# The last two chunks of the last expert's weight go into the first token tiles by a path of their own; filler matmuls, one program body per engine, fifteen small extra loads

## The chip, the core and the metric

The kernel runs on one core of one Trainium2 chip. Its engines are TensorE (PE in the profile; PEld is its weight loads), VectorE (DVE), ScalarE (ACT), GpSimd (POOL) and SyncE (SP), each with a program of its own. Data move between HBM and the on-chip memory SBUF by sixteen DMA engines. Loads are issued by POOL (queue q0 in the profile), the stores of the result by SP (queue q1), and programs are fetched over queue q8. The metric is the device time in microseconds of one execution; lower is better.

## The reference, cut to what matters

Attention comes first, then a mixture of experts in which 32 slots (8 experts of 4) each take a softmax-weighted mean of all 4608 tokens, and each token takes a softmax-weighted mean of the 32 slots' outputs.

```python
x = attention(q, k, v)                  # [4608, 512]: sliding window in heads 0-3, dilated in 4-7
logits = x @ phi                        # [4608, 32]
d = softmax(logits, over tokens)
slot_input = (d.T @ x).reshape(8, 4, 512)
for e in range(8):
    h = relu(slot_input[e] @ w1[e])     # [4, 1024]
    slot_out[e] = h @ w2[e]             # [4, 512]
c = softmax(logits, over the 32 slots)
out = c @ slot_out                      # [4608, 512]
```

## The kernel before

The kernel is written as a list of operations, each with its engine, what it reads and writes, a guessed cost and a key. `Prog.schedule` orders them on a model of the engines: at each step it takes the engine that can start first and, of that engine's operations that could start within 0.12 us of the earliest, the one with the lowest key. POOL and SP keep the order in which the operations were written. `Prog.emit` then walks that order and writes each engine's program, with semaphore waits where an operand comes from elsewhere; before the change, each operation is a body of its own, opened by a decorator call.

Attention runs over 8 units `u` (two batches by one kind of head each). POOL loads q, k, v of a unit with a cast to bf16 (line 396), PE transposes them (lines 520, 525), ACT copies them to `TT` (L544), and scores, exponentials, masks and products follow (L562 to L657). After each second unit come the logits (L671), their exponentials `expT` (slots on 128 partitions, tokens along them; L676) and the slots' sums in the PSUM bank `psA`, bank 7 of eight (L715). The pool `psum` hands out the other seven banks, singly or in three pairs.

The sixteen weights `w10`..`w17`, `w20`..`w27` (each 2 MB in float32, 1 MB as stored in bf16) are loaded by POOL too (`wload`, L425), into buffers `WD`, then into `stg` and `TT` once those are free. The last, `w27`, is loaded in two parts, row chunks 0 to 5 and 6 and 7 of its eight chunks: a chunk has 128 of the 1024 rows, one on each partition, and all 512 columns.

The last stage is a chain. `psA` is copied and folded (L757, L762, L767), the first expert layer is 64 matmuls of 512 columns (L782), ReLU gives `h_sb` (L789, L792), eight transposes and four copies give `hT` (L800, L809). Row sums for the second softmax come from L819 and `rtok` (L824). The second layer, L840, accumulates each expert's four slots in a PSUM pair `sp_`, 32 output partitions for a pair of experts, in two halves of 256 columns. `so_sb` is its scaled copy (L854 on DVE, L858 on ACT). Then 18 tiles of 256 tokens each: two matmuls of 512 columns (L879), one scaled copy each on ACT (L882) and DVE (L885) to a float32 buffer laid over old weight buffers, and one store of 512 KB by SP (L890).

`filler(n)` makes an operation of `n` matmuls of 512 columns whose result nobody reads. `schedule` may place one where PE's model is idle for over 0.4 us within the stretch `FILL`, in model time. `FILL = (125.0, 0)` is an empty stretch.

Of the kernel before, what the change touches and what calls it, by code (L numbers as in the profile page):

```python
# [22 lines left out]
HALO = 32  # L23
FILL = (125.0, 0)

# [84 lines left out]
class Prog:  # L110
# [6 lines left out]
    def op(self, e, fn, r=(), w=(), a=(), alloc=(), cost=0.5, key=0.0, mode="f",  # L117
           sem=None, nbytes=0, after=()):
        o = Op(e, fn, cost, key, mode)
        deps = list(after)  # L120
        for b in r:
            deps += b.ready
        for b in w:
            b.fresh()
            deps += b.prev
        for b in a:
            deps += b.prev
        seen = set()
        for d in deps:
            if d.id not in seen:  # L130
                seen.add(d.id)
                o.deps.append(d)
        for b in r:
            b.reads.append(o)
        for b in list(w) + list(a):
            b.ready.append(o)
        o.wr = [b for b in list(w) + list(a) if b.pool is not None]
        for b in list(r) + list(w) + list(a):
            if b.pool is not None and b not in o.touch:
                b.left += 1  # L140
                o.touch.append(b)
        o.alloc = list(alloc)
        o.sems = sem
        o.bytes = nbytes
        self.ops.append(o)
        return o
# [102 lines left out]
    def emit(self, nc, eng_of):  # L249
        ctr = {e: [nc.alloc_semaphore("c_" + e), 0] for e in ("pe", "act", "dve", "pool", "sp")}  # L250
        known = {e: {} for e in ctr}
        for o in self.order:

            @eng_of[o.e]
            def _(eng, o=o):
                e = o.e
                evs = {}
                hist = [h for t in o.wr for h in t.hist]
                for d in o.deps + hist:
                    if d.e == e == "pe":  # L260
                        continue
                    sem, val = d.ev
                    if val > evs.get(sem.num, (None, 0, None))[1]:
                        evs[sem.num] = (sem, val, d)
                if e == "pool" and o.sems is None and ctr[e][1]:
                    evs[ctr[e][0].num] = (ctr[e][0], ctr[e][1], None)
                kn = known[e]
                todo = sorted(evs.values(), key=lambda x: -(x[2].end if x[2] is not None else 0))
                for sem, val, d in todo:
                    if kn.get(sem.num, 0) >= val:  # L270
                        continue
                    eng.wait_ge(sem, val)
                    kn[sem.num] = max(kn.get(sem.num, 0), val)
                    if d is not None:
                        for k_, v_ in d.snap.items():
                            if kn.get(k_, 0) < v_:
                                kn[k_] = v_
                inst = o.fn(eng)
                if o.sems is not None:
                    for i_ in inst:  # L280
                        i_.then_inc(o.sems.sem, 16)
                        o.sems.val += 16
                    o.ev = (o.sems.sem, o.sems.val)
                else:
                    inst.then_inc(ctr[e][0], 1)
                    ctr[e][1] += 1
                    o.ev = (ctr[e][0], ctr[e][1])
                o.snap = dict(kn)
                o.snap[o.ev[0].num] = o.ev[1]


def bass_dilated_sliding_attn__then__soft_moe_slots_kernel(
# [14 lines left out]
    def sb(name, shape, dt=BF16):  # L307
        return A(nc.sbuf_tensor(name, shape, dt))

    NPT, NVN, NXB, NXT, NET = 6, 5, 5, 4, 2  # L310
    WD = sb("WD", [128, 7, 4096])
    stg = sb("stg", [128, 3, 9216])
# [23 lines left out]
    hT = sb("hT", [128, 2, 8, 4, 32])  # L336
    so_sb = sb("so_sb", [128, DM])

    ps = A(nc.psum_tensor("ps", [128, 8, 512], F32))
# [3 lines left out]
    one = [[i] for i in range(7)]  # L343
    psum = Pool(7, {1: [[6]] + one[:6], 2: [[0, 1], [2, 3], [4, 5]]})

# [7 lines left out]
    def tile(pool, size=1):  # L353
        t = Buf(pool)
        t.size = size
        return t

    def sbt(t):
# [20 lines left out]
    b_expT, b_expX = [Buf() for _ in range(B)], Buf()  # L379
    b_siT, b_h, b_hT, b_so = Buf(), [Buf(), Buf()], [Buf(), Buf()], [Buf(), Buf()]  # L380

    PACE = 13.1
# [4 lines left out]
    def load_unit(u):  # L387
        bp, ty, s = u // 2, u % 2, u % 3

        def f(g):  # L390
# [8 lines left out]
            return res  # L399
        op("pool", f, w=[b_stg[s]], cost=3.5, sem=s_u[s], nbytes=96 * 2 * 4608 * 4)  # L400

# [259 lines left out]
    def st_L(b, u):  # L661
# [49 lines left out]
        def pe3(t):  # L711
# [7 lines left out]
            return i_  # L719
        op("pe", pe3, r=[et, xb0, xb1], a=[b_acc], cost=0.35, mode="c", key=k0 + 4.0)  # L720

# [28 lines left out]
    wload("w26")  # L750
    wload("w27", ((0, 6), (6, 8)))

# [3 lines left out]
    op("dve", lambda vv: vv.reciprocal(rcs[:], rcs[:]), w=[b_rcs], cost=0.1, key=K1)  # L756
    op("dve", lambda vv: vv.tensor_copy(psA_sb[:], psA), r=[b_acc], w=[b_psA], cost=0.65, key=K1)  # L757
    fo = tile(psum, 1)
# [57 lines left out]
    def rsum(t):  # L816
# [8 lines left out]
       cost=0.2, key=K1 + 1)  # L825

    sp_ = tile(psum, 2)
    b_sp = [Buf(), Buf()]
    first = True
    for es_ in ((0, 1, 2, 3), (4, 5, 6), (7,)):  # L830
        for lo, hi_ in ((0, 6), (6, 8)):
            for h_ in range(2):
                pbs = [pb for e in es_ for l2, h2, pb in HOME[f"w2{e}"][1].parts
                       if l2 < hi_ and h2 > lo]

                def pe(t, es_=es_, lo=lo, hi_=hi_, h_=h_):
                    for cc in range(lo, hi_):
                        for e in es_:
                            j, hi = e % 4, e // 4
                            i_ = t.matmul(pair(sp_)[32 * j:32 * j + 32, h_, 0:256],  # L840
                                          hT[:, hi, cc, j, :],
                                          w2v[e][:, cc, 256 * h_:256 * h_ + 256],
                                          start=(hi == 0 and cc == 0), stop=(hi == 1 and cc == 7))
                    return i_
                last_ = op("pe", pe, r=[b_hT[0], b_hT[1]] + pbs, alloc=[sp_] if first else [],
                           a=[sp_, b_sp[h_]], cost=0.12 * (hi_ - lo), mode="c",
                           key=K1 + 2 + es_[0] + (0.5 * h_ + 0.2 * (lo > 0)))
                for e in es_:
                    HOME[f"w2{e}"][1].reads.append(last_)
                first = False  # L850
    for h_ in range(2):
        sl = slice(256 * h_, 256 * h_ + 256)
        if h_ == 0:
            op("dve", lambda vv, sl=sl: vv.tensor_scalar(so_sb[:, sl], pair(sp_)[:, 0, 0:256],  # L854
                                                         rcs[:, 0:1], None, op0=AluOp.mult),
               r=[b_sp[0], b_rcs], w=[b_so[0]], cost=0.35, key=K1 + 20)
        else:
            op("act", lambda ac, sl=sl: ac.activation(so_sb[:, sl], pair(sp_)[:, 1, 0:256],  # L858
                                                      ACTF.Copy, scale=rcs[:, 0:1]),
               r=[b_sp[1], b_rcs], w=[b_so[1]], cost=0.4, key=K1 + 20)  # L860

    for o_ in P.ops[-2:]:
        o_.touch.append(sp_)
        sp_.left += 1

    osts = []
    for ap, b in b_home[:9]:
        t32 = ap.bitcast(F32).rearrange("p (n j f) -> p n j f", n=2, j=2)
        for n_ in range(2):
            osts.append((t32[:, n_], b))  # L870
    for o in range(NOG):
        po = tile(psum, 2)
        ost, hb = osts[o]
        ob = Buf()
        ob.prev = list(hb.ready + hb.reads)

        def pe(t, o=o, po=po):
            for j in range(2):
                i_ = t.matmul(pair(po)[:, j, :], tok[o][:, j], so_sb[:], start=True, stop=True)  # L879
            return i_  # L880
        op("pe", pe, r=b_so + b_expT, w=[po], alloc=[po], cost=0.45, key=K1 + 30 + o)
        op("act", lambda ac, o=o, po=po, ost=ost: ac.activation(  # L882
            ost[:, 0, :], pair(po)[:, 0, :], ACTF.Copy, scale=rtok[:, 2 * o:2 * o + 1]),
            r=[po, b_rtok], a=[ob], after=ob.prev, cost=0.6, key=K1 + 30 + o)
        op("dve", lambda vv, o=o, po=po, ost=ost: vv.tensor_scalar(  # L885
            ost[:, 1, :], pair(po)[:, 1, :], rtok[:, 2 * o + 1:2 * o + 2], None,
            op0=AluOp.mult), r=[po, b_rtok], a=[ob], after=ob.prev, cost=0.6, key=K1 + 30 + o)
        so = DmaSem(nc, f"s_out{o}")
        s_out.append(so)
        op("sp", lambda e, o=o, ost=ost: [e.dma_start(  # L890
            out[256 * o:256 * o + 256, :].rearrange("(p j) f -> p j f", j=2), ost)],
            r=[ob], cost=0.1, sem=so, nbytes=524288, key=K1 + 30 + o)

# [58 lines left out]
```

## Time and profile before

| | |
|---|---|
| Device time, median of 3 runs | 183.03 us (182.87 to 183.22) |
| Profiled execution, its own span, first to last instruction | 181.2 us |
| Around the span, by the median | 1.8 us |
| Mean granted clock of TensorE | 0.922 |
| Busy: PE, PEld, DVE, ACT, POOL | 128.8, 96.6, 112.9, 93.1, 35.8 us |
| Read from HBM, written to it | 61.93 MB, 9.44 MB |

Times in the profile are microseconds from the start of the span. A profile page shows busy shares in forty equal slices, the DMA queues, the chain of work that ended last (each step followed back to what released it), and groups of instructions by source line. No time of the profiled execution beyond its span is recorded, so the median stands for it. Bytes in the DMA rows are counted as stored: a load that casts float32 to bf16 reads twice what they show.

### The profile page before, as it was taken

Reading aid. Unit: us, or ns where it says so; the run is one execution under the profiler, and the core shown is the slowest. Engines: PE = TensorE matmul, PEld = TensorE weight load, DVE = VectorE, ACT = ScalarE, POOL = GpSimd, SP = SyncE. Lnnn points to the kernel's source line nnn. Section 1 sums busy time; section 2 is a strip of 40 time slices with the busy share of each in tenths; the row PEclk is TensorE's granted clock in tenths of the full one; section 3 lists DMA queues with packets and bytes.
Section 4 is the critical chain, followed back from the end, with each engine's and each line's share of the span. In section 5 each row is a group of like instructions: output and inputs, shape, how many; then the busy total and the mean of one; then the engine's idle time right before and its main releaser. Section 6 shows DMA issues by size and latency. Waiting matters only on the chain.

```text
span 181.2 us, 5690 instructions
## 1 busy us (share of the span) xinstructions
PE 128.8 (71%) x2551; PEld 96.6 (53%) x2552; DVE 112.9 (62%) x257; ACT 93.1 (51%) x135; POOL 35.8 (20%) x72
## 2 busy tenths in 40 slices
PE   0018868877988988988887998876958984993000
PEld 0018658665778777778766767755544573210000
DVE  6830794893687799687599579699430201996000
ACT  2006867953775975775785765682400101995000
POOL 7990704303400700800200200204000000000000
PEclk9999999998899999999999999998795799998555
DMA  5999999999999999999999999999999981699995
GB/s 80 210 208 220 207 219 212 216 215 216 221 203 218 208 222 208 219 211 218 212 212 220 208 221 212 217 217 215 219 212 219 211 171 23 242 400 404 408 403 230
DMA packets 7896, 40.80 MB, mean 225 GB/s; under 512 B 1856, under 2 KB 1856, under 8 KB 4416
## 3 DMA queue, kind: packets, MB, share of 16 engines
q0 software_dynamic: 4752, 30.94, 82.6%
q1 hardware_dynamic: 3120, 9.50, 13.4%
q8 instruction: 20, 0.33, 0.7%
q14 instruction: 4, 0.03, 0.0%
HBM read 61.93 MB, written 9.44 MB: 394 GB/s over the span
## 4 chain that ended last, share of the span: by engine, by line
DVE 26%; DMA 25%; PE 23%; ACT 8%; POOL 6%; issue 3%; DVEq 0%; POOLq 0%
DMA TT<-in_moe_w_dram 15%; DMA stg<-in_v_dram 10%; DVE XB L627 8%; DVE PT L577 6%; DVE WD L885 5%; ACT PT L569 5%; POOL stg L396 4%; PE ps L671 4%; PE ps L520 3%; DVE VN L592 3%; PE ps L587 3%; PE ps L525 3%; PE ps L562 2%; PE ps L644 2%; ACT TT L544 2%
## 5 line engine op out<-in xcount | busy, mean ns | idle before, releaser
L544 ACT ACTIVATE TT<-ps 128x864 f32<-128x864 f32 x32 | 28.5, 894 | 31.4 <-PE ps L525 22.5
L569 ACT ACTIVATE PT<-ps 128x768 bf16<-128x768 f32 x48 | 36.6, 815 | 5.7 <-PE ps L562 5.4
L627 DVE TENSOR_TENSOR XB<-ps,RV 96x768 bf16<-96x768 f32 x32 | 30.3, 947 | 0.7
L525 PE MATMUL ps<-ident,stg 96*64 96x96 bf16 x576 | 17.0, 219 | 17.5 <-DMA stg<-in_v_dram 13.2
L525 PEld LDWEIGHTS ps<-ident,stg 96*64 96x64 bf16 x576 | 14.9, 119 | 19.1 <-DMA stg<-in_v_dram 13.4
L592 DVE COPY VN<-ps 128x768 bf16<-128x768 bf16 x32 | 17.6, 548 | 9.6 <-PE ps L587 9.5
L616 PE MATMUL ps<-VN,PT 128*128 128x65 bf16 x384 | 17.6, 194 | 2.9 <-DVE PT L577 1.4
L656 DVE COPY XT<-ps 128x576 bf16<-128x576 bf16 x17 | 10.1, 596 | 12.2 <-PE ps L644 12.1
L396 POOL DMA_DIRECT2D stg<-in_q_dram x16 | 8.4, 528 | 45.3 <-PE ps L525 23.3
L616 PEld LDWEIGHTS ps<-VN,PT 128*128 128x128 bf16 x384 | 14.3, 98 | 5.5 <-DVE PT L577 2.0
L587 PE MATMUL ps<-ident,TT 128*128 128x128 bf16 x192 | 16.5, 224 | 0.7 <-DVE VN L592 0.5
L562 PE MATMUL ps<-TT 64*128 64x96 bf16 x384 | 15.4, 205 | 2.1 <-ACT TT L544 1.0
L644 PE MATMUL ps<-ident,XB 96*128 96x96 bf16 x192 | 13.6, 215 | 3.6 <-DVE XB L627 3.6
L520 PE MATMUL ps<-ident,stg 96*128 96x96 bf16 x288 | 14.9, 206 | 0.1
L577 DVE TENSOR_TENSOR PT<-PT,mask_d 128x768 bf16<-128x768 bf16 x24 | 13.0, 545 | 1.1 <-ACT PT L569 0.6
L644 PEld LDWEIGHTS ps<-ident,XB 96*128 96x128 bf16 x192 | 10.5, 103 | 5.9 <-DVE XB L627 4.9
L587 PEld LDWEIGHTS ps<-ident,TT 128*128 128x128 bf16 x192 | 11.1, 99 | 4.5 <-DVE VN L592 1.4
L520 PEld LDWEIGHTS ps<-ident,stg 96*128 96x128 bf16 x288 | 13.0, 98 | 0.3 <-ACT PT L569 0.3
L562 PEld LDWEIGHTS ps<-TT 64*128 64x128 bf16 x384 | 9.7, 95 | 5.9 <-ACT PT L569 1.4
L577 DVE TENSOR_TENSOR PT<-PT,mask_p 128x768 bf16<-128x768 bf16 x24 | 12.6, 539 | 0.0
L657 ACT ACTIVATE XT<-ps 128x576 bf16<-128x576 bf16 x15 | 9.8, 650 | 3.6 <-PE ps L644 3.3
L879 PE MATMUL ps<-so_sb,expT 128*128 128x512 bf16 x35 | 10.3, 384 | 1.5 <-ACT so_sb L858 0.8
(75 smaller groups left out, 165.2 us busy)
## 6 DMA issues: line engine op xcount, KB each, us to landing
WD<-in_moe_w_dram POOLq DMA_DIRECT2D x7, 1024.0 KB, 27.6
out_dram<-WD SPq DMA_DIRECT2D x14, 512.0 KB, 6.4
stg<-in_moe_w_dram POOLq DMA_DIRECT2D x6, 1024.0 KB, 22.7
stg<-in_q_dram POOLq DMA_DIRECT2D x16, 288.0 KB, 17.1
stg<-in_k_dram POOLq DMA_DIRECT2D x16, 288.0 KB, 18.9
stg<-in_v_dram POOLq DMA_DIRECT2D x16, 288.0 KB, 21.0
TT<-in_moe_w_dram POOLq DMA_DIRECT2D x2, 1024.0 KB, 21.7
out_dram<-stg SPq DMA_DIRECT2D x4, 512.0 KB, 6.3
```

What stands on the lines that cost most here:

```text
L396: res.append(g.dma_start(stg[32 * t + bpar:32 * t + 32:2, s, :].rearrange("r (x f) -> r x f", x=2), rows.rearrange("(x r) f -> r x f", x=2)))
L520: i_ = t.transpose(bankb2(pt, a)[:, 96 * kk:96 * kk + 96], two[:, j // 2, c, :], ident[0:96, 0:96])
L525: i_ = t.transpose(bankb2(pt, a)[64 * hx:64 * hx + 64, 96 * kk:96 * kk + 96], src[:, hx, c, :], ident[0:96, 0:96])
L544: return ac.activation(d, sv, ACTF.Copy)
L562: i_ = t.matmul(pair(sc)[:, hx, QB * x:QB * x + QB], win(u, 1, h01, blk_, bpar)[64 * hx:64 * hx + 64], win(u, 0, h01, blk_, bpar)[64 * hx: ...
L569: op("act", lambda ac: ac.activation(sbt(pt)[:, 0:768].rearrange("p (x n) -> p x n", x=2), pair(sc)[:, :, 0:384], ACTF.Exp, scale=SCALE), ...
L577: return dv.tensor_tensor(p_, p_, m.unsqueeze(1).to_broadcast([128, 2, 384]), AluOp.mult)
L587: i_ = t.transpose(bankb(pv)[:, 128 * m:128 * m + 128], win(u, 2, h01, m, bpar), ident[:, :])
L592: op("dve", lambda dv: dv.tensor_copy(sbt(vn)[:, :, :, 0:64], bankb(pv)[:, 0:768].rearrange("p (m x d) -> p m x d", m=6, x=2)), r=[pv], w= ...
L616: i_ = t.matmul(pair(po)[:, bk, 65 * po_:65 * po_ + 65], sbt(pts[i])[:, o_:o_ + 128], sbt(vn)[:, m, half, 0:65], start=True, stop=True)
L627: op("dve", lambda dv: dv.tensor_tensor(sbt(xb)[:].rearrange("p m (x h d) -> p h x m d", x=2, h=2)[:, h01], pv()[:, :, :, 0:64], sbt(rv)[: ...
L644: i_ = t.transpose(bankb(px)[:, QB * m:QB * m + QB], sbt(xb)[:, m, 128 * x:128 * x + 128], ident[0:QB, 0:QB])
```

## The change

1. `w27` is loaded in four parts, chunks 0 to 3, 4 and 5, 6, and 7. Behind it POOL issues fifteen loads of n by n numbers, n from 1 to 15, into a small tensor `mk` that nobody reads or waits for.
2. For the first 512 tokens (tiles 0 and 1) the contribution of chunks 6 and 7 no longer passes through `so_sb`. Expert 7's ReLU output for those chunks, scaled by a mask for its slots and by `rcs`, becomes `h7`; `G[c]` is `h7`'s chunk c times `expT` for the 512 tokens. Tile o is then `so_sb` without chunks 6 and 7 (`first(None, ..)`), plus `G[0]` times chunk 6, plus `G[1]` times chunk 7. The keys of these PE operations are 22, 22.2 and 22.4, plus o, plus 0.1 for the second matmul group j (all on top of 1000). Tile 0 is copied out and stored in two halves of 256 KB, each copied by ACT and DVE together; tile 1 is copied as before.
3. Chunks 6 and 7 are added to `sp_` afterwards, and a second copy of the slots' outputs, `so_all`, serves tiles 2 to 17: partitions 0 to 95 are copied by POOL from `so_sb`, 96 to 127 by DVE and ACT from PSUM.
4. `FILL` becomes (116.0, 149.0), so filler matmuls are placed.
5. PSUM bank 7 joins the pool once `psA` has been copied, as a fourth pair with bank 6.
6. `emit` works out waits and counts first, and then opens one body per engine.

```diff
-FILL = (125.0, 0)
+FILL = (116.0, 149.0)
...
     def emit(self, nc, eng_of):
-        for o in self.order:
-            @eng_of[o.e]
-            def _(eng, o=o):
...
+        for e in ctr:
+            @eng_of[e]
+            def _(eng, e=e):
+                for o, waits in todo_of[e]:
+                    for sem, val in waits:
+                        eng.wait_ge(sem, val)
+                    inst = o.fn(eng)
...
-    psum = Pool(7, {1: [[6]] + one[:6], 2: [[0, 1], [2, 3], [4, 5]]})
+    psum = Pool(8, {1: [[6]] + one[:6], 2: [[0, 1], [2, 3], [4, 5], [6, 7]]})
...
-    wload("w27", ((0, 6), (6, 8)))
+    wload("w27", ((0, 4), (4, 6), (6, 7), (7, 8)))
+    mk = sb("mk", [15, 136])
+    for n_ in range(1, 16):
+        o_ = sum(range(n_))
+        op("pool", lambda g, n_=n_, o_=o_: [g.dma_start(mk[0:n_, o_:o_ + n_], moe_w2[7, 0:n_, 0:n_])],
+           cost=0.3, sem=DmaSem(nc, f"s_mark{n_}"), nbytes=1024)
...
+    op("dve", lambda vv: vv.tensor_scalar(sbt(h7)[:, 0:256].rearrange("p (f c) -> p f c", c=2),
+                                          h_sb[:].rearrange("p (f c) -> p f c", c=8)[:, :, 6:8],
+                                          m7[:, 0:1], None, op0=AluOp.mult),
+       r=[b_m7] + b_h, w=[h7], alloc=[h7], cost=0.3, key=K1 + 1.5)
+    for c in range(2):
+        gp = tile(psum, 1)
+        op("pe", lambda t, c=c, gp=gp: t.matmul(bank(gp)[:, 0:NG], sbt(h7)[:, c:256:2], expT[:, 0:NG],
+                                                start=True, stop=True),
...
-    for es_ in ((0, 1, 2, 3), (4, 5, 6), (7,)):
-        for lo, hi_ in ((0, 6), (6, 8)):
-            for h_ in range(2):
+    for es_, lo, hi_ in (((0, 1, 2, 3), 0, 8), ((4, 5, 6), 0, 8), ((7,), 0, 4), ((7,), 4, 6)):
+        for h_ in range(2):
+            ffn2(es_, lo, hi_, h_, K1 + 2 + es_[0] + 0.1 * lo + 0.02 * h_)
...
+    op("pool", lambda g: g.tensor_copy(so_all(0, 96), so_sb[0:96, :]), r=b_so, w=[b_soa[0], t_soa],
+       alloc=[t_soa], cost=1.0, key=K1 + 21)
...
+                    for h_ in range(2 if o == 0 else 1):
+                        sl = slice(256 * h_, 256 * h_ + 256) if o == 0 else slice(0, 512)
+                        d_ = pair(po)[:, h_, 0:256] if o == 0 else pair(po)[:, j, :]
+                        if c is None:
+                            i_ = t.matmul(d_, tok[o][:, j], so_sb[:, sl], start=True, stop=False)
+                        else:
+                            i_ = t.matmul(d_, Gt(o, c)[:, j], w2v[7][:, 6 + c, sl],
+                                          start=False, stop=c == 1)
...
+    first(None, K1 + 22)
+    first(0, K1 + 22.2)
+    first(1, K1 + 22.4)
+    for h_ in range(2):
+        ffn2((7,), 6, 8, h_, K1 + 22.8 + 0.01 * h_)
...
+        if o == 0:
+            for j in range(2):
+                ob = Buf()
+                for h_ in range(2):
+                    op(("act", "dve")[h_], lambda en, o=o, j=j, h_=h_, ev=ev: ev(en, o, j, h_),
+                        r=[po[j], b_rtok], a=[ob], after=prev, cost=0.35, key=K1 + 24.5 + j)
+                store(o, j, ost, ob, K1 + 24.5 + j)
+            continue
```

## The prediction

> **What bounds the kernel now.** I read the busy shares by slice first: the DMA engines are full from the start to 147 us, nearly idle for some six, and full again to the end.
>
> ```profile
> DMA  5999999999999999999999999999999981699995
> GB/s 80 210 208 220 207 219 212 216 215 216 221 203 218 208 222 208 219 211 218 212 212 220 208 221 212 217 217 215 219 212 219 211 171 23 242 400 404 408 403 230
> q8 instruction: 20, 0.33, 0.7%
> ```
>
> So the time is loads, a hole, stores. Only the ends of the two streams and the hole between them can pay. The chain of waits, from 150 us, says what fills the hole.
>
> ```profile
> 123.25 27.74 DMA TT<-in_moe_w_dram
> 151.03 1.94 PE ps L840 x16
> 152.99 0.48 ACT so_sb L858
> 153.75 0.39 PE ps L879
> 154.17 9.31 DVE WD L885 x14
> ```
>
> The six-chunk part of `w27` lands at 150.99; sixteen matmuls, one scaled copy, two matmuls and one copy later SP issues the first store. The timeline has that issue; the stretches have the stream it starts.
>
> ```profile
> 155.01 15.62 SPq L890 DMA_DIRECT2D out_dram<-WD  x14
> ...
> 155.00:156.00 1.00, 0.95 (x4) 0.21 (x4) 1.00 (x2) 1.00 (x3) 0.00 (x0) 1.00 0.15 61
> 160.00:179.00 19.00, 4.44 (x15) 0.80 (x14) 6.11 (x10) 5.53 (x9) 0.00 (x0) 0.67 1.02 405
> 179.00:179.20 0.20, 0.00 (x0) 0.00 (x0) 0.00 (x0) 0.00 (x0) 0.00 (x0) 0.50 0.64 246
> 179.20:180.40 1.20, 0.00 (x0) 0.00 (x0) 0.00 (x0) 0.00 (x0) 0.00 (x0) 0.50 0.06 24
> ```
>
> The last numbers are granted clock, DMA share, GB/s. With 0.15 us of traffic before 156, the first bytes move at 155.85, 0.85 us after the issue. Then 9.44 MB at 404 GB/s are 23.36 us, to 179.21. But from 179.2 to 180.3 a share of 0.06, one engine of sixteen, still works. The DMA views of that stretch and of 160.0 to 161.2 tell why:
>
> ```profile
> DMA  0000300030000300003000030000300030000000
> ...
> q8 instruction: 1, 0.02, 4.8%
> ```
>
> Seven packets of 4 KB, one after another, and earlier one program fetch taking 4.8% of sixteen engines for 1.2 us: 0.92 us of one engine. Seven packets at 0.15 us are 1.05 us. I read this as one fetch that pushed one engine's stores back, and the kernel's end with them.
>
> **The change part by part**, against the profiled span of 181.2 us; the median, 183.03, is 1.83 above it.
>
> *Landing.* All bytes and their order stay. Chunks 4 and 5 end where chunks 0 to 5 ended, 150.99, plus eight more packets per engine. Stores of 4 KB take 0.169 us each (13.4% of the span over 144 per engine) against 0.162 by bytes at 25.3 GB/s per engine, so a packet costs 0.01; at most 0.05, an estimate. I take +0.1: 151.1. The old second part landed 0.7 us after the first (issues 123.27 and 123.81, 27.7 and 27.9 us to landing), so chunk 7 comes at 151.9.
>
> *First store.* Of L840's sixteen matmuls (1.92 us; one lasts 0.27, so the pitch is 0.11) eight, chunks 0 to 3, now run before the landing and four, chunks 6 and 7, later. The four left end at 151.14 + 3 x 0.11 + 0.27 = 151.74; ACT's copy, 0.47, ends at 152.25; PE starts 0.07 later, 152.32 (before, 153.47 to a weight load at 153.52). A matmul of 512 columns lasts 0.38, of 256 0.27, so 256 columns are 0.11 of pitch. Keys 22, 22.2, 22.4 put tile 0 first, twelve matmuls of 256: the tenth ends first half's sum at 152.32 + 9 x 0.11 + 0.27 = 153.58 (chunk 7 is long there). The copy of 256 columns takes 0.48, issue 0.09: 154.18 against 155.01, 0.83 earlier. The other half follows at 154.66.
>
> *Second tile.* This gives it back. After tile 0 (153.64) come the four matmuls of chunks 6 and 7 into `sp_` (154.08), then tile 1's six of 512 columns, pitch 0.22: 154.08 + 5 x 0.22 + 0.38 = 155.56. Before, a tile took two. The copy takes 0.74, so SP issues at 156.42 and bytes move at 157.27. Tile 0's 512 KB are 1.30 us of the stream, so the queue runs dry for about a microsecond. Before, tile 1's bytes moved at 155.85 + 1.30 = 157.15. From here seventeen tiles remain in both kernels: +0.12 us. Tile 2 is no wall: its matmuls end at 156.0, its copies at 157.1, half a tile ahead of need. So the direct path itself is worth about nothing, +0.12; 0.83 of gain if tile 1 were in time, 0.3 more of loss with one more `issue` like that between 153.47 and 153.75.
>
> *Fillers.* They move the program fetches. PE has 2551 matmuls and 2552 weight loads; 20 fetches make one per 255, so the fetches are PE's and come by position in its program. The last one comes at 160.4 to 161.2, when L879, at four instructions per 0.66 us since 153.52, has run 42 of its 72: 30 before the end. By the code PE gets 16 more matmuls (32 instructions), some six waits, and fillers: its idle stretches from 119 to 137 us, some 5.5 us in the timeline, hold 20 to 25 at 0.216, or 40 to 50 instructions. The program is some 85 longer ahead of its end, so the same place lies 115 before the end. Tiles 2 to 17 are 64 of these, tile 1, chunks 6 and 7 and tile 0 another 12, 8 and 24, together 108. The fetch therefore moves to the start of tile 0's matmuls, 152 or a little sooner, with nothing in transit until 155.03. Then no store waits behind it: -1.05 us. With fewer than some 10 fillers it meets the stores again: 0.
>
> The page "Runtime: NRT & Kernel Launch" (Instruction fetch mechanics) says a block boundary's cost is mostly hidden; by that this term would be 0 and the forecast 183.2. The row differs: 0.92 us of one engine, and one engine late.
>
> *Fillers' own cost.* They stand in order before real work on PE, 0.22 us each at full clock, 0.43 at half. What hides a delay: PE idles from 149.28 to 151.03, and experts 4 to 6 wait for `w26`, landing at 147.0. So 0 here; without that cover at most one misjudged gap per group, some 0.1 to 0.4 us. If they hold the clock, L782's 6.2 us at half shrink towards 3.5, worth 0 behind the same landing.
>
> *The rest.* G's two matmuls, the copies to G, `h7` and the mask run at 144 to 147, where PE waits for `hT` and DVE and ACT are idle from 145.5: 0; uncovered, 0.7 for one 512-column copy. The fifteen loads issue on POOL, 15 x 0.54 = 8.1 us after 125.4, with nothing behind them but the copy to `so_all`, at 152.3. They stand behind the last weight on each queue: 22 small packets per engine with their counts. The phi load's 32 per engine landed in 2.2 us, so under 1.5 us, in the empty hole: 0; 1.5 on the slowest engine if stores met them. POOL's copy of 96x512 is nearest to L454's 128x960, 1.1 us: ready at 153.5, wanted at 155.4. One body per engine: no branch shows in the trace and neighbouring operations of one engine follow within 0.05 us, so 0; at most one `issue` of 0.3 us either way. Bank 7 only serves the new tiles.
>
> Sum: +0.12 - 1.05 = -0.93: the last bytes at 179.35, span 180.3, time 182.1.
>
> **Rivals.** *The fetch stays among the stores, or the late engine has another cause.* Then only +0.12 is left: 183.15, no change. For: fetches at 134, 148 and 160 are unevenly spaced. Against: 0.92 and 1.05 us agree, and it is one engine.
>
> *Both pay.* If tile 1's chain is about a microsecond shorter than I sum, the stream runs from 155.03 without a gap: 183.03 - 0.83 - 1.05 = 181.15.
>
> *Slower: the clock halves in the tail.* Stretches of 3.4 us from 122.1 on show it:
>
> ```profile
> 122.10:125.50 3.40, 1.92 (x46) 1.55 (x42) 3.37 (x8) 1.31 (x2) 2.11 (x4) 1.00 0.99 207
> 125.50:128.90 3.40, 3.11 (x21) 2.09 (x22) 2.24 (x6) 0.99 (x4) 0.00 (x0) 0.51 1.09 227
> ...
> 149.30:152.70 3.40, 1.67 (x16) 1.47 (x16) 0.00 (x0) 0.00 (x0) 0.00 (x0) 1.00 0.19 35
> ```
>
> After 1.92 us of work in 3.4 the clock was halved for the next 3.4; after 1.67 at 149.3 to 152.7 it was not. The new PE has about as little there (0.9 + 0.5 + 0.4), and a warm first layer leaves a wait for `w26` ahead of it. Halved from 152.75 to 156.2, tile 0 ends at 155.5 and tile 1's sum at 157.3: 1.75 us later, 183.03 + 1.75 + 0.12 - 1.05 = 183.85; 184.9 with the fetch in place. It decides from about 1 us of delay on. The page "TensorE: Matmul & The Clock Gate" (HAM oscillation) asks for an idle gap over about 3.4 us; here no gap before 125.5 exceeded 1 us and the clock fell, so I keep the rival; by the page it would be nil.
>
> **How the numbers follow.** Forecast 182.1 (181.7 to 182.6 by itself): 0.45. No change, 183.15: 0.20. Both pay: 0.08. Halved clock or delays like it: 0.27. Two runs are told apart from about 0.2%, 0.37 us. Faster 0.53, same 0.20, slower 0.27. The range reaches from both paying to the halved clock with some of the fetch: 181.1 to 184.2.
>
> **What would show it.** Right: no single engine after the stores' common end; no q8 packet after 155; first store near 154.2, a dry stretch of about a microsecond, second tile's issue near 156.4; four L840 matmuls after the landing near 151.1. Wrong: stores continuous from 154.9 (both pay), a clock of 0.5 after 149 (slower), a landing off 151 by over 0.5 us, or a late engine without a fetch.

## The result, and the profile after

The changed kernel takes 182.19 us (median of 20 executions, 181.69 to 183.27). The kernel before, run beside it, takes 183.25 (20 executions). The ratio is 0.9953, with a 95% interval of 0.9935 to 0.9972: faster, by about half a per cent. Ratios, here and below, leave out executions that took over 1.5% longer than the fastest of the same kernel. The forecast was 182.1. The profiled execution has a span of 180.5 us (before 181.2) and a mean granted clock of 0.956 (before 0.922).

The page of the kernel after comes first: the granted clock, the DMA share and the rate in forty slices of 4.5 us, and the fetch queue.

```profile
PEclk9999999999999999999999699999999999999655
DMA  5999999999999999999999999999999993499998
GB/s 72 196 219 206 220 210 212 218 212 216 214 214 219 211 216 214 214 216 212 216 213 212 218 214 218 216 216 214 212 221 212 216 188 53 155 404 406 403 406 318
q8 instruction: 20, 0.33, 0.7%
```

The shape is the same: loads, a hole of about 6 us, stores at some 404 GB/s. Still 20 fetches, but the last slice moves 318 GB/s where before it moved 230. The chain of waits of the kernel after runs through the hole. Its columns are start, length, engine and line. L888 is `ffn2`'s matmul (before L840), L906 the copy to `so_sb` (before L854/L858), L941 and L943 `first` without and with a chunk, L1001 and L1002 the copies of finished tiles (before L882/L885). "issue" is time in which the engine waited for nothing that the profile shows.

```profile
151.10 0.04 issue
151.15 0.62 PE ps L888 x4
151.77 0.03 issue
151.80 0.49 DVE so_sb L906
152.29 0.14 issue
152.43 0.60 PE ps L941 x4
153.03 0.87 PE ps L943 x8
153.90 0.54 PE ps L888 x4
154.44 0.54 PE ps L941 x2
154.98 0.88 PE ps L943 x4
155.85 0.03 issue
155.88 8.65 DVE WD L1001 x13
```

Chunks 4 and 5 land at 151.10, and four matmuls are left where before there were sixteen. Tile 0 follows, then chunks 6 and 7 into `sp_`, then tile 1, as the keys order them. SP's timeline has the stores: the first at 154.29 (before 155.01), then a pause until 156.70.

```profile
154.29 6.55 SPq L977 DMA_DIRECT2D out_dram<-WD  x7
...
156.70 0.33 SPq L977 DMA_DIRECT2D out_dram<-WD  x1
```

The first line is a group of seven stores; the second is tile 1's store alone, from a narrower window. The stretches of the same kernel show what the stream makes of that; the last three columns are granted clock, DMA share and GB/s.

```profile
155.00:155.25 0.25, 0.25 (x3) 0.10 (x2) 0.12 (x1) 0.05 (x1) 0.00 (x0) 1.00 0.45 172
155.25:156.50 1.25, 1.25 (x7) 0.59 (x6) 0.62 (x1) 0.62 (x2) 0.00 (x0) 1.00 1.00 375
156.50:157.50 1.00, 1.00 (x6) 0.45 (x5) 1.00 (x3) 1.00 (x3) 0.00 (x0) 1.00 0.04 12
157.50:179.50 22.00, 7.17 (x25) 1.27 (x23) 9.66 (x15) 8.42 (x15) 0.00 (x0) 0.74 1.02 405
179.50:180.00 0.50, 0.00 (x0) 0.00 (x0) 0.00 (x0) 0.00 (x0) 0.00 (x0) 0.50 0.04 8
```

Tile 0's 512 KB move, the queue is dry for about 0.95 us, and the rest moves without a break to 179.5, where all sixteen engines stop together. The share of 0.06 that one engine kept up for more than a microsecond in the kernel before is gone. And the last fetch, which had begun among the stores between 160.4 and 161.2, now begins between 150.4 and 151.6, in the DMA view of that stretch:

```profile
q8 instruction: 1, 0.02, 10.7%
```

That is 0.107 x 16 x 1.2 = 2.05 us of one engine, in the last load packets and the empty hole behind them. A view counts a packet whole in the stretch in which it begins; by the packet's own times this fetch runs from 150.99 to 153.04, and the one of the kernel before from 161.02 to 161.95. No fetch comes after it.

### The profile page after: what moved, and what is told of

Read it like the earlier page. It is cut to its first block, busy times and chain, and to the rows that moved or that the text cites. A ratio compares the mean times of both kernels' runs of the same rounds, so it can differ in the third digit from the quotient of the medians.

```text
span 180.5 us, 5811 instructions
## 1 busy us (share of the span) xinstructions
PE 133.5 (74%) x2597; PEld 99.2 (55%) x2597; DVE 114.9 (64%) x263; ACT 93.7 (52%) x138; POOL 44.9 (25%) x90
## 4 chain that ended last, share of the span: by engine, by line
PE 31%; DVE 26%; DMA 19%; ACT 9%; issue 4%; POOL 2%; DVEq 0%; POOLq 0%
DMA TT<-in_moe_w_dram 14%; DVE XB L644 7%; DVE PT L594 7%; PE ps L542 6%; DMA stg<-in_v_dram 5%; DVE WD L1001 5%; PE ps L537 5%; PE ps L688 4%; ACT TT L561 4%; ACT PT L586 4%; DVE VN L609 4%; PE ps L604 4%; PE ps L661 3%; PE ps L579 3%; PE ps L633 3%
## 5 line engine op out<-in xcount | busy, mean ns | idle before, releaser
L542 PE MATMUL ps<-ident,stg 96*64 96x96 bf16 x576 | 17.9, 225 | 17.1 <-DMA stg<-in_v_dram 13.0
L542 PEld LDWEIGHTS ps<-ident,stg 96*64 96x64 bf16 x576 | 15.8, 124 | 18.6 <-DMA stg<-in_v_dram 13.0
L661 PE MATMUL ps<-ident,XB 96*128 96x96 bf16 x192 | 12.9, 208 | 3.2 <-DVE XB L644 3.0
L661 PEld LDWEIGHTS ps<-ident,XB 96*128 96x128 bf16 x192 | 9.8, 99 | 6.0 <-DVE XB L644 4.9
L442 POOL DMA_DIRECT2D stg<-in_moe_w_dram x6 | 3.2, 534 | 39.4 <-PE ps L537 26.4
```

The lines of the kernel that those rows point to most:

```text
L542: i_ = t.transpose(bankb2(pt, a)[64 * hx:64 * hx + 64, 96 * kk:96 * kk + 96], src[:, hx, c, :], ident[0:96, 0:96])
L661: i_ = t.transpose(bankb(px)[:, QB * m:QB * m + QB], sbt(xb)[:, m, 128 * x:128 * x + 128], ident[0:QB, 0:QB])
```

## The experiments

Two theories were set against each other. F: the gain is the program fetch, which the extra PE instructions move out of the store stream. D: the gain is the earlier first store by the direct path. Beside them stood the fillers' effect on the clock, the fifteen small loads and the single body per engine. Each ratio below is to the kernel before, run beside it on the same chip; 0.002 is 0.37 us.

**Only the fillers, in the kernel before.**

```diff
-FILL = (125.0, 0)
+FILL = (116.0, 149.0)
```

> The kernel before with FILL = (116.0, 149.0) and nothing else: 38 filler matmuls, 76 PE instructions more ahead of the last tiles. Theory F (the gain of the change is the program fetch leaving the stores): the last fetch moves from 160 to 151-154 us, no engine works alone behind the stores, about 1.0 us faster than before (ratio 0.994 to 0.996), without any direct path. Theory D (the gain is the earlier first store): no gain, ratio 0.999 to 1.001, first store still near 155.0. Theory C (the gain is the warm clock): part of the gain, and the landing of the last weight or the sixteen matmuls behind it come earlier by the time gained.

Measured: 182.22 us (181.54 to 183.01, 12 executions), ratio 0.9964 (0.9940 to 0.9988). The stretch that placed no filler now placed 38. The last fetch came at 148 to 150, and the stores ended together at 180.1. But the fillers were not free here. PE's and SP's timeline of the profiled execution, which took 182.78:

```profile
149.41 2.62 PE L899 MATMUL ps<-mask_p,ident 128*128 128x512 bf16 x6
151.96 1.92 PE L840 MATMUL ps<-TT,hT 128*32 128x256 bf16 x16
155.94 0.35 SPq L890 DMA_DIRECT2D out_dram<-WD  x1
```

Six fillers at half clock, 0.44 us each, ran past the landing of the first part of `w27` at 150.70: the sixteen matmuls began at 151.96 and not at 151.03, and the first store was 0.93 later than before. Without a late engine (-1.05) and with 0.93 of delay the span should be 0.1 shorter, and it is: 181.1 against 181.2. The twelve times lie in two groups of six, 181.5 to 182.0 and 182.5 to 183.0; the upper one holds the profiled execution. That the lower one is the case without fillers in the way fits its size, but no profile shows it.

**Only a shift of PE's program, in the kernel before.** 31 matmuls of 32 columns ahead of everything else on PE, 62 instructions with their weight loads, while PE still waits for its first data. Their result is overwritten later.

```diff
+    def early(t):
+        for _ in range(31):
+            i_ = t.matmul(psA[:, 0:32], ident[:, :], ident[:, 0:32], start=True, stop=True)
+        return i_
+    op("pe", early, r=[b_id], a=[b_acc], cost=0.05 * 31, key=-1.0)
```

> The kernel before with 31 matmuls of 32 columns on PE while it waits for its first load (5 to 12.7 us); their result is overwritten. They shift every later PE instruction by 62 places in the program and do no work near the tail. Theory F: the last fetch falls between 150.5 and 154 us, no late engine, 0.8 to 1.1 us faster (ratio 0.994 to 0.996), the clock still halved at 125 and 136 us as before. Theories D and C: ratio 0.999 to 1.001.

Measured: 181.64 us (181.31 to 181.81, 6 executions), ratio 0.9936 (0.9914 to 0.9957). This kernel does nothing sooner and has 31 useless matmuls more, and it gains as much as the whole change. Its fetch, in the DMA view of 150.5 to 151.0, and its stretches:

```profile
q8 instruction: 1, 0.02, 12.1%
```

```profile
155.70:178.90 23.20, 8.31 (x28) 1.50 (x26) 10.29 (x16) 9.70 (x16) 0.00 (x0) 0.74 1.02 405
178.90:179.00 0.10, 0.00 (x0) 0.00 (x0) 0.00 (x0) 0.00 (x0) 0.00 (x0) 0.50 1.14 451
179.00:180.00 1.00, 0.00 (x0) 0.00 (x0) 0.00 (x0) 0.00 (x0) 0.00 (x0) 0.50 0.01 0
```

0.121 x 16 x 0.5 is 0.97 us of one engine, now ahead of the stores. They end together at 179.0, and the span is 180.0: 1.2 below before, of which 0.12 is a first store at 154.89 in place of 155.01. The clock was not better for it: 0.897 on average (before 0.922), and 0.56 in 122.0 to 125.4. Theory F stands, and what is left to D is small.

**The change without its fillers.**

```diff
-FILL = (116.0, 149.0)
+FILL = (125.0, 0)
```

> The changed kernel with FILL = (125.0, 0): 58 PE instructions fewer. Theory F: the last program fetch moves back to 155.5 to 158 us, into the first stores; most of the gain goes, ratio to before 0.998 to 1.002, and again one engine ends up to 1 us behind the others (less if the packet falls into the dry stretch of about a microsecond ahead of the second tile's store). Theory D: the gain stays, ratio 0.994 to 0.996. Theory C: as F in time, but by a clock of 0.5 in the tail and not by a late engine.

Measured: ratio 1.0038 (1.0002 to 1.0075). The gain is gone. The ratio is of six of the twelve executions, five of 182.6 to 183.4 us and one of 185.2; the other six took 185.4 to 187.3. The only profile is of the longest one, so where the fetch stood in the others is not known, and the expected place, 155.5 to 158, is not confirmed. In the long one PE stood for 2.01 us, an "issue", between the copy to `so_sb` and tile 0, and the clock was halved behind that. The chain and the stretch show it:

```profile
152.34 0.49 DVE so_sb L906
152.83 2.01 issue
154.84 0.80 PE ps L941 x4
155.64 1.71 PE ps L943 x8
```

```profile
155.10:158.50 3.40, 3.40 (x17) 1.84 (x15) 1.06 (x3) 1.05 (x3) 0.00 (x0) 0.50 0.03 13
```

The last fetch came at 164 to 166, and one engine alone worked to the end. What causes the stall is open. The fetch ahead of it ran from 150.61 to 152.72, 2.11 us; but the changed kernel's took 2.05 us in the same place and no such stall followed, so a long fetch by itself does not explain it.

**The change without fillers, but with the shift.** The same as the last, plus the 31 matmuls.

> The changed kernel without fillers, but with the 31 small matmuls at the start: the program position of the fillers without their work near the tail. Theory F: as the changed kernel, ratio to before 0.994 to 0.996, last fetch near 150.5 to 152.5 us, no late engine, although the clock falls at 125 and 136 us as in the kernel before. Theory C: no gain, 0.999 to 1.001. Theory D: 0.994 to 0.996 too.

Measured: 181.97 us (181.74 to 183.16, 10 executions), ratio 0.9966 (0.9943 to 0.9988). The fetch is at 150 to 152 again, the stores end together at 179.1, the span is 180.0. So what the fillers give is their number of instructions, not a warm clock: the clock was halved in places between 123 and 140 and it cost nothing that shows. This kernel has the direct path, and its first store is at 153.83; the shifted kernel before has none, and its first store is at 154.89. SP's timelines, this kernel first:

```profile
153.83 6.54 SPq L983 DMA_DIRECT2D out_dram<-WD  x7
154.89 5.38 SPq L896 DMA_DIRECT2D out_dram<-WD  x6
```

The spans of these two executions are equal, and the medians are no better with the direct path (181.97 against 181.64). A lead of 1.06 us at the first store is worth nothing at the end.

**The single body per engine, in the kernel before.** Only `emit` is replaced by the new one.

```diff
-        for o in self.order:
-            @eng_of[o.e]
-            def _(eng, o=o):
+        for e in ctr:
+            @eng_of[e]
+            def _(eng, e=e):
+                for o, waits in todo_of[e]:
```

> The kernel before with the new emission, one body per engine, and nothing else. The instructions that run are the same, so theory F has the last fetch at 160 us, the late engine and a ratio of 0.998 to 1.002. If the many bodies cost time (branches, fetches of their own): fewer or earlier fetches, shorter issue gaps, ratio below 0.997.

Measured: 182.93 us against 183.06, ratio 0.9987 (0.9959 to 1.0015). The last fetch begins between 161.5 and 162.0, about 0.6 later than before, as does the first store of this execution (155.57 against 155.01), and the one late engine is there as before:

```profile
179.70:181.00 1.30, 0.00 (x0) 0.00 (x0) 0.00 (x0) 0.00 (x0) 0.00 (x0) 0.50 0.07 25
```

**The change without the fifteen small loads.**

```diff
-    for n_ in range(1, 16):
-        ...
-        op("pool", lambda g, n_=n_, o_=o_: [g.dma_start(mk[0:n_, o_:o_ + n_], moe_w2[7, 0:n_, 0:n_])],
```

> The changed kernel without its fifteen small loads. If they are hidden, as the prediction has it: ratio to before as the changed kernel, 0.993 to 0.997, landing of the second part of the last weight within 0.2 us of 151.1. If their packets behind the last weight cost (or bring) time: the landing or the first stores move by 0.3 to 1.0 us, to 0.990 or 1.000.

Measured: 182.11 us (181.73 to 182.77, 12 executions), ratio 0.9948 (0.9924 to 0.9972), the same as with them. The profiled execution was the longest of them, and its stretches show the clock falling in the tail, which neither profile of before and after has:

```profile
145.10:148.50 3.40, 1.16 (x33) 1.10 (x36) 0.00 (x0) 0.00 (x0) 0.00 (x0) 1.00 0.99 187
148.50:151.90 3.40, 3.40 (x33) 2.17 (x26) 0.00 (x0) 0.00 (x0) 0.00 (x0) 0.50 0.43 76
```

PE had been idle for 3.0 us until `w26` landed at 147.30, and its matmuls then ran at half clock past the landing of chunks 4 and 5 at 151.06. There the copy to `so_sb` was at 152.34 and the first store at 154.83, 0.5 us later than in the changed kernel.

**The change, with the fetch shifted back into the stores.** 80 matmuls of 32 columns ahead of everything, 160 instructions: by F the fetch that the change had moved to 151 goes far ahead, and the next one comes in at 160 or so.

```diff
+    def early(t):
+        for _ in range(80):
+            i_ = t.matmul(psA[:, 0:32], ident[:, :], ident[:, 0:32], start=True, stop=True)
+        return i_
+    op("pe", early, r=[b_id], a=[b_acc], cost=0.05 * 80, key=-1.0)
```

> The changed kernel with 80 matmuls of 32 columns on PE before its first load lands; their result is overwritten. 160 more PE instructions put the fetch after the last one of now 22 to 39 instructions before the end, where the last one was before the change. Theory F: a program fetch near 160 us again, one engine working alone for about 1 us behind the stores, the whole gain lost: 0.8 to 1.1 us slower than the changed kernel, ratio to before 0.998 to 1.002. Theory D (first store): as the changed kernel, 0.993 to 0.997, since nothing of the tail changes.

Measured: 183.31 us against 183.06, ratio 1.0011 (0.9987 to 1.0035). The first store is where it was, 154.22, and the gain is gone. The page, the DMA view of 161.5 to 162.0, the stretches, and the DMA view of the end, from 179.7 on:

```profile
q8 instruction: 21, 0.34, 0.7%
```

```profile
q8 instruction: 1, 0.02, 11.6%
```

```profile
157.50:179.50 22.00, 7.09 (x24) 1.26 (x22) 9.59 (x15) 8.34 (x15) 0.00 (x0) 0.71 1.02 403
179.50:180.70 1.20, 0.00 (x0) 0.00 (x0) 0.00 (x0) 0.00 (x0) 0.00 (x0) 0.50 0.07 27
```

```profile
DMA  0000300000300003000003000030000030000000
```

One fetch of 0.93 us (0.116 x 16 x 0.5) and, 18 us later, one engine that works alone for 1.2 us, packet after packet: the picture of the kernel before, made by position in the program alone.

**The kernel before, shifted by a whole fetch.** 128 early matmuls, 256 instructions, about the 255 from one fetch to the next. If the fetch counts by its place, the last one comes back to where it was; if early matmuls themselves make the kernel faster, it is faster.

> The kernel before with 128 early matmuls of 32 columns in place of e2's 31: 256 PE instructions, one whole fetch. Theory F: one fetch more, and the last one again near 160 us, where it was; the late engine is back and the gain of e2 gone, ratio 0.999 to 1.004 (one more packet of 0.9 us among the loads may cost up to 0.3 us). If early work on PE helps by itself: 0.994 or less, as e2.

Measured: 182.87 us against 182.93, ratio 0.9984 (0.9959 to 1.0009). 21 fetches, the last at 160 to 162, and the late engine:

```profile
155.80:179.10 23.30, 8.28 (x28) 1.51 (x26) 10.26 (x16) 9.67 (x16) 0.00 (x0) 0.78 1.02 404
179.10:180.40 1.30, 0.00 (x0) 0.00 (x0) 0.00 (x0) 0.00 (x0) 0.00 (x0) 0.50 0.07 25
```

One fetch more among the loads costs nothing that shows. 62 instructions gain 0.64%, 256 gain nothing: it is the place.

**Tile 1 in halves, too.** The dry stretch ahead of tile 1 takes back what the first store gains. Here tile 1 is summed, copied and stored in two halves of 256 KB like tile 0, each half in a PSUM pair of its own, and their PE operations come half by half.

```diff
-    PO = [[tile(psum, 2), tile(psum, 2)], tile(psum, 2)]
+    PO = [[tile(psum, 2), tile(psum, 2)] for _ in range(2)]
...
-                po = PO[0][j] if o == 0 else PO[1]
+                po = PO[o][j]
...
-                    for h_ in range(2 if o == 0 else 1):
+                    for h_ in range(2):
...
+                       key=key + 0.1 * j if o == 0 else K1 + 23 + 0.4 * (key - K1 - 22) + 0.5 * j,
...
-        if o == 0:
+        if o < 2:
```

> The changed kernel with tile 1 summed, copied and stored in two halves of 256 KB as tile 0 is, first half first (12 PE instructions more). If the dry stretch of 0.95 us behind tile 0 is what eats the direct path's gain: first half's store issued at 155.8 in place of 156.70, traffic without a gap from 155.1, 0.5 to 0.8 us faster than the changed kernel, ratio to before 0.990 to 0.994. If the stores end on something else (a late engine, a slower rate with 2 KB packets): ratio 0.994 to 0.997.

Measured: 181.33 us (181.08 to 182.17, 8 executions), ratio 0.9919 (0.9890 to 0.9948). SP's timeline and the stretches:

```profile
154.09 2.49 SPq L978 DMA_DIRECT2D out_dram<-WD  x4
```

```profile
154.90:156.40 1.50, 1.50 (x12) 0.96 (x11) 1.21 (x4) 1.18 (x3) 0.00 (x0) 1.00 0.94 350
156.40:156.50 0.10, 0.10 (x2) 0.06 (x1) 0.10 (x1) 0.10 (x1) 0.00 (x0) 1.00 0.51 185
156.50:178.50 22.00, 7.81 (x29) 1.71 (x26) 10.25 (x16) 9.01 (x16) 0.00 (x0) 0.75 1.02 404
178.50:179.50 1.00, 0.00 (x0) 0.00 (x0) 0.00 (x0) 0.00 (x0) 0.00 (x0) 0.50 0.02 4
```

Four stores are out by 156.6, the stream has only a tenth of a microsecond at half rate at 156.4, and it ends at 178.5 instead of 179.5. Of that 1.0 us, 0.2 is the earlier first store of this execution (154.09 against 154.29, as chunks 4 and 5 landed at 150.82 and not at 151.10); the rest, about 0.8, is most of the 0.95 us of dry stretch in the changed kernel. So the direct path pays once its second tile is in time.

**Both improvements, without the fillers.** Tile 1 in halves, `FILL` empty, and the 31 early matmuls in the fillers' place.

> Tile 1 in two halves, no fillers, 31 matmuls of 32 columns at the start in their place: both gains without filler matmuls on PE's way. By theory F and the first-store gain of e10: last fetch at 150 to 152 us, no late engine, stores without a gap from about 155; ratio to before 0.988 to 0.993, at least as fast as e10. If the fillers' warm clock was worth something in the tail: 0.993 to 0.996.

Measured: 181.16 us (181.05 to 181.52, 6 executions), ratio 0.9900 (0.9871 to 0.9928). The last fetch is at 150 to 152, the stores end together at 178.8. It is the lowest of all the kernels here; its interval ends below that of the changed kernel, and it overlaps with the last one's.

## Why the prediction was right, step by step

**Fillers move the fetch, -1.05: right, and shown.** The last fetch was to come at "152 or a little sooner"; it began at 150.99, and no engine was late. The shift alone gives the gain (0.9936), the shift back takes it away (1.0011), a whole fetch of shift does nothing (0.9984). The count was a little off and it did not matter: 29 fillers were placed and not 20 to 25, and the old fetch began at 161.02 with 21 of PE's matmuls and weight loads to go, not 30. The new one began with 116 to go, where the sum had 115. The packets' own times show what the fetch does to the stores: while the one of the kernel before lasts, 15.3 store packets are in flight on average, against 16.2 in the stream a microsecond behind it. So one engine's place in the stream is empty for 0.93 us. That it is this engine which ends late is inferred from the like sizes; the trace does not name the engines.

The page "Runtime: NRT & Kernel Launch" of the Trainium skill (Instruction fetch mechanics) says that a boundary's cost is mostly hidden. For PE that holds here: one fetch more among the loads cost nothing that shows (0.9984). For the DMA engine that carries the fetch it does not: with a fetch among the stores the span was 1.2 us longer (181.2 against 180.0 with the shift, 0.12 of it from the first store) or 1.0 (181.5 with the shift back against 180.5).

**Direct path, +0.12 net: the mechanism was right, and one term was too small.** The steps up to the first store hold within 0.11 us: landing 151.10 (forecast 151.1), four matmuls to 151.77 (151.74), first store 154.29 (154.18), second 154.74 (154.66). The lead of 0.72 at the first store was given back in a dry stretch of 0.95, as forecast ("about a microsecond"). The mis-sized term is tile 1's chain: its sum ended at 155.85 against 155.56, its store was issued at 156.70 against 156.42, and bytes moved at 157.5 against 157.27. 0.11 of that came with PE's start, since the copy-to-PE step was an "issue" of 0.14 where 0.07 was taken and the copy itself was done 0.04 later. The rest is the 22 matmuls from there: 3.42 us measured against 3.24 by pitches. By the chain, tile 0's twelve took 1.47 against 1.32 and the four of chunks 6 and 7 took 0.54 against 0.44; why is not shown. Tile 1's bytes therefore came 0.35 later than before (157.15), not 0.12. The common end of the streams, 179.5 against 179.35, is 0.15 from the forecast.

So the span fell by 0.7 (181.2 to 180.5) and not by 0.93. That the median lies within 0.09 of the forecast is in part luck: the profiled execution, at 182.26, is itself 0.16 above it.

**Fillers' own cost, 0: right here, by a margin that is thin.** In the changed kernel PE had been idle for 0.24 us when chunks 4 and 5 landed. In the kernel before with fillers, six of them at half clock kept PE from the sixteen matmuls for 0.93 us. That is more than the 0.1 to 0.4 by which the prediction bounded it without cover, because the gap was misjudged and the clock was half as well.

**Small loads, one body, bank 7, G and `h7`: 0 each.** The first two are shown (0.9948 with the loads left out, 0.9987 for the body alone). POOL issued the loads in 7.48 us, from 126.60 to 134.1 (8.1 forecast), and its copy to `so_all` took 0.61 us at 152.42. Bank 7 and the work for `G` were not tried by themselves; the chain does not run through `G`.

**Rivals.** "The fetch stays" is excluded by the DMA view. "Both pay" failed at the place that the prediction named, tile 1's chain, and it is what the version with tile 1 in halves turns into: 181.33, where the rival was priced at 181.15. "The clock halves in the tail" did not happen in the changed kernel's profiled execution, whose stretches before the tail are these:

```profile
144.10:147.50 3.40, 1.95 (x67) 1.65 (x70) 0.29 (x1) 0.00 (x0) 0.00 (x0) 1.00 1.03 203
147.50:150.90 3.40, 2.88 (x56) 2.17 (x56) 0.00 (x0) 0.00 (x0) 0.00 (x0) 1.00 0.78 125
```

Elsewhere it did happen, and by the wait that the rival named, the one for `w26` behind a first layer at full clock. In the version without small loads PE was idle for 3.0 us in that wait, and the clock was halved from 148.5 on. With tile 1 in halves it was idle for 2.95 us, and the clock was halved from 147.1 on:

```profile
143.70:147.10 3.40, 0.45 (x20) 0.17 (x8) 0.00 (x0) 0.00 (x0) 0.00 (x0) 1.00 1.04 207
147.10:150.50 3.40, 3.39 (x53) 2.51 (x54) 0.00 (x0) 0.00 (x0) 0.00 (x0) 0.51 0.82 135
```

The first store was 0.5 us later than in the changed kernel in the one case and 0.2 earlier in the other, where the rival was priced at 1.75. That price was for a halving from 152.75 to 156.2; these began earlier and were over by 151.9. So the rival is real, but it lives in the spread from one execution to the next, and it may be what the three times above 182.7 of the changed kernel are; no profile shows that. How little work makes the clock fall stays open: in these stretches of 3.4 us it fell after 0.45 and 1.16 us and not after 1.95, but in the kernel before it fell after 1.92 and not after 1.67.

## What to carry to other kernels

Where a kernel ends in a stream that fills all DMA engines, look for program fetches inside it and for one engine that finishes alone: counting the instructions from fetch to fetch tells how many, at a place where the engine idles anyway, move the fetch out of the stream. An earlier first transfer is worth only as much as the second one keeps up; sum the chain to the second store before counting the gain. A change with many parts can owe its whole gain to a side effect of one of them, here the bare number of instructions, and the cheapest test is that side effect alone.

## What was not expected of the hardware

62 instructions that compute nothing, at the start of a PE program of some 5100, are worth 1.2 us of the span 150 us later. A fetch takes 0.93 to 0.96 us of one DMA engine among the stores, and 0.89 to 0.98 at the end of the loads in most profiles, but 2.05 us there in the changed kernel, 2.11 in the version without fillers and 2.19 in the last one. All three have the fifteen small loads; two more that have them too, the one with the shift and without fillers and the one with tile 1 in halves, took 0.94 and 0.93. Which of the sixteen engines a fetch uses is not seen. Without fillers and without a shift, PE stalled for 2.01 us right before the first tile in the one profile there is of it, and seven of its twelve executions were 2 to 4 us longer than the rest; this has no explanation yet.
